# A one-core attention and expert kernel: the order of its first loads and of its first two batches rewritten

## The chip, the core and the metric

The kernel runs on one core of one Trainium2 chip. TensorE (PE in the rows) multiplies matrices into PSUM, VectorE (DVE), ScalarE (ACT) and GpSimd (POOL) compute, and SyncE (SP), ScalarE and GpSimd issue DMAs. Each engine works through its own list of instructions in the order in which the program wrote them, and waits on semaphores for the others. The metric is the device time of one execution in microseconds (us). Before the change it was 331.68 us, the median of three runs that span 331.52 to 332.45.

## The reference, cut to what matters

```python
q, k, v: (8, 12, 448, 64)                       # batch, heads, tokens, head_dim
q_n, k_n = rmsnorm(q, g_q), rmsnorm(k, g_k)     # x / sqrt(mean(x*x) + 1e-6) * g
scores = q_n @ k_n.T / sqrt(64)                 # 448 x 448 for each head
attn = softmax(scores)
x = (attn @ v) -> rows of 12 heads * 64: (3584, 768)
e = token_ids * 2654435761 % 8                  # expert of each token
out[token] = relu(x[token] @ w1[e]) @ w2[e]     # w1 768 x 1024, w2 1024 x 768
```

## The kernel before, in words

The attention runs as 48 steps: 8 batches of 6 steps, and a step (s) is two heads that lie 6 apart in their batch. For a step TensorE makes four pieces of transposed scores (`sc:s.0` to `sc:s.3`; the first three are 128x896, the last 128x448), ScalarE exponentiates each (`exp:s.j`, lines 660 and 663), TensorE multiplies with v (`av:s.0` to `av:s.2`), and VectorE takes reciprocals and scales (`rec`, `x`). Steps 1 and 2, 3 and 4, 6 and 7 and so on share one unit of preparation; steps 0 and 5 are prepared alone.

Preparation of a unit: squares of q and k (`sqq`, `sqk`, line 375 on VectorE; with the mark `@A` line 373 on ScalarE), sums of the squares by TensorE against an identity (`sumq`, `sumk`, line 387), the rest of the sum on VectorE (`redq`, `redk`, line 402), a logarithm and an exponential on ScalarE that give the inverse root (`ln` line 406, `er` line 412), the normalizing product on VectorE (`nq`, `nk`, line 435), transposes on TensorE (`Tq`, `Tk`, lines 595 to 607) and the copy out of PSUM into `qT` and `kT` (lines 623 to 629; `@A` puts it on ScalarE). Squares, sums and inverse roots are made by groups of units: group 0 is step 0, group 1 steps 1 and 2, group 2 steps 3, 4 and 5, groups 3 and 4 are batch 1 (steps 6, 7 and steps 8 to 11), group 5 is batch 2. `v:c` (line 444) copies a chunk of v into the form that `av` reads; chunk 0 is step 0, chunk 1 steps 1 and 2, chunk 2 steps 3 to 5.

PSUM has three double banks `sc_ps` that score pieces take in turn, one bank `qkT_ps`, and the `av_ps` banks. Sums and transposes go to `qkT_ps`, or with the mark `@S` to an `sc_ps`; a bank's next user waits until the last reader of the one before is done.

Loads: q, k and v of step 0 and step 5 come as float32 (step 0 through SP, ACT and POOL; step 5 through SP), all else through POOL's queue as a cast to 16 bits. `load_pairs` (line 317) loads q or k of one unit or one batch in one DMA; `load_v(s, n)` (line 306) loads v of n steps in four DMAs, of which the two with 256 elements a row have 96 KB and the two with 192 elements 72 KB for three steps. Eight of POOL's DMAs can be under way: each waits for the landing of the eighth before it, as its semaphores show.

The order of the first two batches is a text of tokens that `emit` reads from left to right; each token appends its instructions to the lists of the engines that it needs. So the text sets the order on every engine at once. From batch 2 on, another text (`steady`) is used six times over, and after attention come the eight experts. `spin:n` is n idle multiplies of 448 columns of zeros (line 827) into a bank that nobody reads.

```python
        emit("""
            zero:0 zero:1 zero:2 zero:6 zero:7 spin:11 sqk:0.0 zero:3 sqq@A:0.0 sumk@S:0.0
            redk:0.0 sumq@S:0.0 ln:0.1.2 redq:0.0 er:0.1.2 ln:0.0.1 er:0.0.1 sqk@A:1.0
            ...
        """, None)
```

Of the kernel before, what the change touches and what calls it, by code (L numbers as in the profile page):

```python
# [20 lines left out]
def kernel(  # L21
# [243 lines left out]
    with tc.manual_schedule(), \  # L265
# [640 lines left out]
        emit("""
            zero:0 zero:1 zero:2 zero:6 zero:7 spin:11 sqk:0.0 zero:3 sqq@A:0.0 sumk@S:0.0
            redk:0.0 sumq@S:0.0 ln:0.1.2 redq:0.0 er:0.1.2 ln:0.0.1 er:0.0.1 sqk@A:1.0
            gain:0 spin:2 nk:0 spin:4 gain:1 Tk@S:0 nq:0 sumk@S:1.0 gain:2 sqq:1.0 Tq@S:0
            redk:1.0 sumq:1.0 kT:0 redq:1.0 qT@A:0 sc:0.0 ln:1 er:1 sc:0.1 spin:5 exp:0.0  # L910
            nk:1 Tk@S:1 sc:0.3 nq:1 Tq:1 sqk:2.0.0 kT:1 qT:1 exp:0.1 sqq:2.0.0 v:0
            sqk@A:2.0.1 sc:0.2 exp:0.3 sumk@S:2.0 sc:1.0 sqq@A:2.0.1 exp:0.2 exp:1.0
            sumq:2.0 redk:2.0 av:0.0 redq:2.0 sc:1.2 av:0.1 v:1 sc:1.3 ln:2 er:2 av:0.2
            sc:1.1 nq:3 rec:0 exp:1.2 exp:1.3 Tq@S:3 exp:1.1 nk:3 sc:2.0 Tk:3 x:0 exp:2.0
            sc:2.1 exp:2.1 qT:3 kT:3 sc:2.2 av:1.0 exp:2.2 sc:2.3 av:1.1 av:1.2 sqk:3.0
            sc:4.0 exp:2.3 nk:5 sumk:3.0 rec:1 exp:4.0 sc:3.0 x:1 sc:3.1 av:2.0 redk:3.0
            av:2.1 sqk:4.0 exp:3.0 nq:5 sumk:4.0 v:2 sc:3.2 av:2.2 redk:4.0 sqq:3.0 rec:2
            exp:3.1 Tk@S:5 sc:3.3 kT:5 x:2 sumq:3.0 exp:3.2 sc:4.3 sc:4.2 exp:3.3 redq:3.0
            exp:4.3 ln:3 er:3 sc:4.1 exp:4.2 av:3.0 sqk:4.1 Tq:5 exp:4.1 sqq:4.0 av:3.1 qT:5
            sumk@S:4.1 nq:6 av:3.2 nk:6 redk:4.1 sc:5.0 rec:3 sumq:4.0 sc:5.3 sc:5.1 exp:5.0  # L920
            exp:5.3 redq:4.0 sqq:4.1 x:3 Tk:6 exp:5.1 Tq@S:6 kT:6 sumq@S:4.1 redq:4.1 qT@A:6
            av:4.0 av:4.1 ln:4 sc:5.2 av:4.2 er:4 exp:5.2 sc:6.0 sqk:5.0 v:4 sc:7.0 sumk:5.0
            exp:6.0 rec:4 sc:6.3 x:4 av:5.0 av:5.1 exp:7.0 exp:6.3 nq:8 sc:7.3 redk:5.0 nk:8
            exp:7.3 v:3 Tq:8 sc:6.1 av:5.2 qT:8 sc:6.2 Tk@S:8 rec:5 sqq:5.0 exp:6.1 sc:7.1
            sumq:5.0 x:5 exp:6.2 av:6.0 sc:7.2 exp:7.1 exp:7.2 kT:8 sc:8.0 sqq:5.1 redq:5.0
            sc:8.1 nq:10 exp:8.0 av:6.1 sumq:5.1 nk:10 redq:5.1 exp:8.1 av:6.2 sc:8.3 rec:6
            Tk:10 x:6 sc:9.0 sc:8.2 exp:8.3 av:7.0 sc:9.3 exp:9.0 kT:10 Tq:10 av:7.1 av:7.2
            sc:9.1 sqk:5.1 qT:10 exp:8.2 rec:7 sc:9.2 x:7 v:5 exp:9.3 exp:9.1 sumk:5.1
            redk:5.1 exp:9.2 sqq:6.0 av:8.0 av:8.1 av:8.2 sc:10.0 sc:10.2 sc:10.1 rec:8 ln:5
            er:5 x:8 nk:12 exp:10.0 sumq:6.0 av:9.0 exp:10.1 sc:10.3 redq:6.0 Tk:12 av:9.1  # L930
            nq:12 av:9.2 kT:12 rec:9 exp:10.2 sc:11.0 exp:10.3 exp:11.0 sc:11.2 exp:11.2
            sc:11.3 x:9 Tq:12 sqq:6.1 av:10.0 av:10.1 sc:11.1 qT:12 nk:14 av:10.2 exp:11.3
            sc:12.0 sumq:6.1 sc:12.2 rec:10 exp:11.1 sc:12.1 x:10 exp:12.0 exp:12.2 redq:6.1
            Tk:14 sc:12.3 sqk:6.0 exp:12.1
        """, None)
# [407 lines left out]
```

## Time and profile before

| | before |
|---|---|
| median of the runs | 331.68 us (331.52 to 332.45, 3 runs) |
| the profiled execution | 332.74 us |
| its span in the trace | 331.1 us |
| TensorE matmul busy | 318.2 us, 96% of the span |
| VectorE busy | 239.3 us, 72% |
| ScalarE busy | 207.5 us, 63% |
| bytes moved by DMA | 65.52 MB, mean 198 GB/s |
| granted TensorE clock, mean | 0.994 |

The span runs from the first to the last instruction of the core; 1.6 us of the profiled execution lie around it. Attention fills the span until about 159 us, the experts the rest. Every time below is counted from the start of the span. The profiled execution is 1.06 us longer than the median of the runs.

### The profile page before, as it was taken

To read this page: it belongs to the slowest core of one execution; us is meant where nothing else is said; L and a number is where in the kernel's file an instruction comes from. 1 tells how busy PE (TensorE), PEld (TensorE's weight loads), DVE (VectorE), ACT (ScalarE), POOL (GpSimd) and SP (SyncE) were. 2 spreads that over 40 slices of the span, in tenths; PEclk is the share of its full clock that TensorE was granted. 3 is DMA by queue.
4 is the path that set the end of the run, shared out by engine and by line. 5 is a ranking of instruction groups with operands and counts; after the bars stand their busy time and mean duration, and the time that the engine had idled before them with its cause. 6 is when DMAs were issued, how large, how long until landed. Compare 5 with 4: busy or idle time off the path is not lost. (4 is left out here: it accounts for less than half of the span.)

```text
span 331.1 us, 8985 instructions
## 1 busy us (share of the span) xinstructions
PE 318.2 (96%) x3765; PEld 219.7 (66%) x3765; DVE 239.3 (72%) x457; ACT 207.5 (63%) x317; POOL 149.5 (45%) x207
## 2 busy tenths in 40 slices
...
GB/s 122 197 202 203 194 242 196 236 200 240 203 240 212 245 225 227 164 70 70 124 152 211 165 207 242 244 264 265 265 272 239 254 253 260 307 174 137 23 48 124
DMA packets 45601, 65.52 MB, mean 198 GB/s; under 512 B 12727, under 2 KB 33423, under 8 KB 45432
## 3 DMA queue, kind: packets, MB, share of 16 engines
...
q10 hardware_dynamic: 160, 0.11, 0.1%
...
## 5 line engine op out<-in xcount | busy, mean ns | idle before, releaser
L660 ACT ACTIVATE expT<-sc_ps 128x896 bf16<-128x896 f32 x144 | 125.1, 960 | 1.0 <-PE sc_ps L637 0.7
L1072 DVE STREAM_TRANSPOSE xT<-kr 32x768 f16<-32x768 f16 (+1 forms) x80 | 73.6, 920 | 25.7 <-DMA kr<-x_scratch,gidx 15.2
L1024 PEld LDWEIGHTS <-h_sb 128*128 128x128 f16 (+1 forms) x512 | 52.2, 104 | 31.3
L1024 PE MATMUL o_ps<-w_sb,h_sb 128*128 128x512 f16 (+3 forms) x384 | 64.2, 326 | 0.0
L1011 ACT ACTIVATE h_sb<-h_ps 128x480 f16<-128x480 f32 (+1 forms) x56 | 31.3, 560 | 48.6 <-PE h_ps L1002 48.6
L1037 POOL DMA_INDIRECT out_dram<-o_sb,gidx x32 | 35.1, 1097 | 57.6 <-ACT o_sb L1034 29.6
L1034 ACT COPY o_sb<-o_ps 128x768 f32<-128x768 f32 (+1 forms) x26 | 20.8, 799 | 54.5 <-PE o_ps L1024 54.5
L230 POOL DMA_INDIRECT kr<-x_scratch,gidx x32 | 32.6, 1020 | 49.3 <-DVE qT L629 37.1
L1002 PEld LDWEIGHTS <-w_sb 128*128 128x128 f16 x300 | 39.8, 135 | 16.4 <-issue 0.7
L1002 PE MATMUL h_ps<-xT,w_sb 128*128 128x480 f16 x240 | 49.4, 366 | 0.3 <-DVE xT L1072 0.3
L637 PE MATMUL sc_ps<-qT,kT 64*128 64x448 f16 x288 | 44.4, 356 | 0.5 <-DVE qT L629 0.4
L678 PEld LDWEIGHTS <-expT 128*128 128x128 bf16 x846 | 36.8, 97 | 9.2 <-DVE x_sb L738 4.4
L678 PE MATMUL av_ps<-v,expT 128*128 128x65 bf16 x828 | 41.5, 193 | 0.1
L306 POOL DMA_DIRECT2D vr<-in_v_dram x36 | 23.7, 670 | 20.8 <-DMA kr<-in_k_dram 11.5
L738 DVE TENSOR_TENSOR x_sb<-av_ps,srec 128x448 f16<-128x448 f32 x47 | 29.3, 623 | 1.3
L663 ACT ACTIVATE expT<-sc_ps 128x448 bf16<-128x448 f32 x48 | 28.4, 595 | 0.1
L387 PEld LDWEIGHTS <-ident 128*128 128x128 f16 x576 | 22.6, 98 | 8.7 <-issue 4.4
L683 PE MATMUL av_ps<-v,expT 128*128 128x130 bf16 x138 | 24.0, 220 | 0.0
L1024 PE MATMUL o_ps<-kr,h_sb 128*128 128x512 f16 (+3 forms) x128 | 21.1, 326 | 0.0
L1002 PE MATMUL h_ps<-xT,qr 128*128 128x480 f16 x96 | 19.8, 366 | 0.5 <-DVE xT L1072 0.5
L637 PEld LDWEIGHTS <-kT 64*128 64x128 f16 x288 | 12.3, 93 | 9.5 <-issue 2.2
...
## 6 DMA issues: line engine op xcount, KB each, us to landing
...
kr<-in_k_dram POOLq DMA_DIRECT2D x7, 672.0 KB, 15.6
qr<-in_q_dram POOLq DMA_DIRECT2D x7, 672.0 KB, 12.9
...
vr<-in_v_dram POOLq DMA_DIRECT2D x14, 192.0 KB, 13.6
```

The source lines that it names most:

```text
L230: nc.gpsimd.indirect_dma_start(out=xg[0:idx.shape[0], :], out_offset=None, in_=x_dram[0:rows, :], in_offset=bass.IndirectOffsetOnAxis(ap=i ...
L637: nc.tensor.matmul(sc[:, hh, :S], lhsT=kT[64 * hh:64 * hh + 64, P * j:P * j + P], rhs=qT[64 * hh:64 * hh + 64, :], start=True, stop=True)
L660: nc.scalar.activation(expT[:, 2 * j:2 * j + 2, :], sc[:, :, :S], AF.Exp, bias=0.0, scale=1.0)
L663: nc.scalar.activation(expT[:, 6, :], sc[:, 0, :S], AF.Exp, bias=0.0, scale=1.0)
L678: nc.tensor.matmul(av[:, 2 * t + hh, :], lhsT=expT[:, tl(hh, j), P * t:P * t + P], rhs=v8[:, i, vs(hh, j), 0:D + 1], start=(hh == 0 and t ...
L683: nc.tensor.matmul(av[:, 2 * t:2 * t + 2, :], lhsT=expT[:, 6, P * t:P * t + P], rhs=v8[:, i, 0::7, 0:D + 1], start=False, stop=False)
L738: nc.vector.tensor_tensor(out=xs[b][:, :, hp * D:hp * D + D], in0=av[:, :, :D], in1=srec[:, :, None].to_broadcast([P, SL, D]), op=ALU.mult)
L1002: nc.tensor.matmul(dst, lhsT=w1v[:, co, fo, :], rhs=src, start=(co == 0), stop=(co == CO - 1))
L1011: nc.scalar.activation(h_sb[:, fo, c0:c1], h_ps[:, :c1 - c0], AF.Relu)
L1024: nc.tensor.matmul(o_ps[d0 > 0][0:w, d0:d1], lhsT=h_sb[:, fo, col * P:col * P + w], rhs=w2_sb[:, fo, d0:d1], start=(fo == 0), stop=(fo == ...
L1037: scat = nc.gpsimd.indirect_dma_start(out=out[:, :], out_offset=bass.IndirectOffsetOnAxis(ap=idx[0:w], axis=0), in_=o_sb[0:w], in_offset=N ...
L1072: nc.vector.transpose(out=dst[32 * m:32 * m + 32, :, g].rearrange("p c k r -> p k c r"), in_=xg[32 * i:32 * i + 32, 0:n, m])
```

## The change

Three things are rewritten, all in the text between the first load and the second batch's end; no instruction's arithmetic is changed.

1. POOL's first loads: q of steps 1 and 2 goes ahead of the identity that POOL builds, and k and q of steps 3 and 4 go ahead of v of steps 0 to 2 (`load_v(0, 3)`).
2. The token text of batches 0 and 1: the same tokens in another order. Some change engine or bank: the squares of step 0's q go from ScalarE to VectorE; step 0's kT goes from VectorE to ScalarE and its qT the other way, and the same for steps 6 and 7; the bank of several sums and transposes changes. In batch 1 the tokens of k's squares stand further back beside what else is done.
3. Idle multiplies: 14, 7 and 5 in place of 11, 2, 4 and 5.

```diff
         load_pairs(k, k_bufs, 0, 1, 0, HP, 2)
+        load_pairs(q, q_bufs, 0, 1, 0, HP, 2)
         make_identity(nc, ident16[:])
-        load_pairs(q, q_bufs, 0, 1, 0, HP, 2)
-        load_v(0, 3)
         load_pairs(k, k_bufs, 0, 3, 2 * PAIR, HP, 2)
         load_pairs(q, q_bufs, 0, 3, 2 * PAIR, HP, 2)
+        load_v(0, 3)
         load_v(3, 3)
...
-            zero:0 zero:1 zero:2 zero:6 zero:7 spin:11 sqk:0.0 zero:3 sqq@A:0.0 sumk@S:0.0
+            zero:0 zero:1 zero:2 zero:6 zero:7 spin:14 sqk:0.0 sqq:0.0 gain:0 sumk@S:0.0
...
```

POOL's list, from k of steps 1 and 2 to v of steps 0 to 2, is this before (`kr_0`, `qr_0` and `vr_0` are the buffers of k, q and v; 128x2x448 is one unit):

```order
L317 DMA kr_0_68<-in_k_dram 128x2x448
masks.py:197 MEMSET ident16_75 128x128
masks.py:199 AFFINE_SELECT ident16_75<-ident16_75 128x128
L317 DMA qr_0_67<-in_q_dram 128x2x448
L306 DMA vr_0_143<-in_v_dram 64x3x256
L306 DMA vr_0_143<-in_v_dram 64x3x192 x2
L306 DMA vr_0_143<-in_v_dram 64x3x256
L317 DMA kr_0_68<-in_k_dram 128x2x448
L317 DMA qr_0_67<-in_q_dram 128x2x448
```

and this after:

```order
L317 DMA kr_0_68<-in_k_dram 128x2x448
L317 DMA qr_0_67<-in_q_dram 128x2x448
masks.py:197 MEMSET ident16_75 128x128
masks.py:199 AFFINE_SELECT ident16_75<-ident16_75 128x128
L317 DMA kr_0_68<-in_k_dram 128x2x448
L317 DMA qr_0_67<-in_q_dram 128x2x448
L306 DMA vr_0_143<-in_v_dram 64x3x256
L306 DMA vr_0_143<-in_v_dram 64x3x192 x2
```

The loads of steps 3 and 4 have passed the four of v; what comes after them in the queue is the same.

VectorE's list, from the squares of q of steps 1 and 2 to the first copy of v, is this before:

```order
L375 TENSOR_TENSOR sq_q_359<-qr_0_67 128x14x16x4
L402 TENSOR_REDUCE ss_366<-sc_ps_341 128x14
L626 TENSOR_SCALAR kT_385<-sc_ps_334,g_col_78 128x512
L402 TENSOR_REDUCE ss_366<-qkT_ps_368 128x14
L435 TENSOR_TENSOR n8_k_147<-kr_0_68,rr_394 128x2x7x64
L435 TENSOR_TENSOR n8_q_146<-qr_0_67,rr_394 128x2x7x64
L375 TENSOR_TENSOR sq_k_427<-kr_0_68 128x14x16x4
L626 TENSOR_SCALAR kT_429<-sc_ps_407,g_col_78 128x1024
L629 COPY qT_431<-qkT_ps_419 128x896
L375 TENSOR_TENSOR sq_q_434<-qr_0_67 128x14x16x4
L444 COPY v8_145<-vr_0_143 128x8x64
L402 TENSOR_REDUCE ss_483<-sc_ps_442 128x22
```

and this after:

```order
L375 TENSOR_TENSOR sq_q_363<-qr_0_67 128x14x16x4
L629 COPY qT_370<-sc_ps_365 128x448
L402 TENSOR_REDUCE ss_372<-sc_ps_346 128x14
L435 TENSOR_TENSOR n8_q_146<-qr_0_67,rr_398 128x2x7x64
L435 TENSOR_TENSOR n8_k_147<-kr_0_68,rr_398 128x2x7x64
L375 TENSOR_TENSOR sq_k_409<-kr_0_68 128x14x16x4
L629 COPY qT_453<-sc_ps_416 128x896
L375 TENSOR_TENSOR sq_q_457<-qr_0_67 128x14x16x4
L402 TENSOR_REDUCE ss_460<-qkT_ps_433 128x22
L626 TENSOR_SCALAR kT_462<-sc_ps_424,g_col_78 128x1024
L444 COPY v8_145<-vr_0_143 128x8x64
```

Step 0's copy out is now that of qT; the copies of steps 1 and 2 come q first, with the squares of q of steps 3 and 4 between them; the copy of v stays last here.

ScalarE's list around its first exponentials is this before (`expT_404` is step 0, `expT_464` step 1):

```order
L660 ACTIVATE expT_404<-sc_ps_390 128x896
L660 ACTIVATE expT_404<-sc_ps_396 128x896
L373 ACTIVATE sq_k_427<-kr_0_68 128x8x16x4
L663 ACTIVATE expT_404<-sc_ps_416 128x448
L373 ACTIVATE sq_q_434<-qr_0_67 128x8x16x4
L660 ACTIVATE expT_404<-sc_ps_438 128x896
L660 ACTIVATE expT_464<-sc_ps_459 128x896
L406 ACTIVATE ss_483<-ss_483 128x2x22
L412 ACTIVATE rr_515<-ss_483 128x2x44
L660 ACTIVATE expT_464<-sc_ps_496 128x896
```

and this after (`expT_400` is step 0, `expT_504` step 1):

```order
L660 ACTIVATE expT_400<-sc_ps_393 128x896
L373 ACTIVATE sq_k_409<-kr_0_68 128x8x16x4
L660 ACTIVATE expT_400<-sc_ps_411 128x896
L373 ACTIVATE sq_q_457<-qr_0_67 128x8x16x4
L660 ACTIVATE expT_400<-sc_ps_450 128x896
L663 ACTIVATE expT_400<-sc_ps_455 128x448
L406 ACTIVATE ss_460<-ss_460 128x2x22
L412 ACTIVATE rr_502<-ss_460 128x2x44
L660 ACTIVATE expT_504<-sc_ps_485 128x896
L663 ACTIVATE expT_504<-sc_ps_500 128x448
```

The logarithm and inverse root of steps 3 to 5 now stand ahead of step 1's first exponential.

## Rows read from the trace of the kernel before

**Rows 1.** Busy time by stretch: length, each engine's busy us, clock, DMA share, GB/s

```profile
25.00:35.00 10.00, 10.00 (x217) 7.60 (x214) 9.89 (x25) 9.88 (x17) 9.59 (x25) 1.00 1.35 201
60.00:80.00 20.00, 20.00 (x368) 14.54 (x365) 18.67 (x39) 20.00 (x33) 6.81 (x10) 1.00 1.28 231
```

**Rows 2.** Timeline of ScalarE: start us, us, what, xcount [idle before it <- releaser]

```profile
12.31 0.23 ACT L406 ACTIVATE ss<-ss 128x28 f32<-128x28 f32 x1 [1.87 <-DVE ss L402]
12.72 1.71 ACT L660 ACTIVATE expT<-sc_ps 128x896 bf16<-128x896 f32 x2
...
17.17 0.92 ACT L660 ACTIVATE expT<-sc_ps 128x896 bf16<-128x896 f32 x1 [0.46 <-PE sc_ps L637]
...
18.75 0.90 ACT L660 ACTIVATE expT<-sc_ps 128x896 bf16<-128x896 f32 x1
...
19.97 3.34 ACT L660 ACTIVATE expT<-sc_ps 128x896 bf16<-128x896 f32 x4
23.16 0.59 ACT L663 ACTIVATE expT<-sc_ps 128x448 bf16<-128x448 f32 x1
23.58 3.40 ACT L660 ACTIVATE expT<-sc_ps 128x896 bf16<-128x896 f32 x4
...
54.89 0.61 ACT L663 ACTIVATE expT<-sc_ps 128x448 bf16<-128x448 f32 x1
```

**Rows 3.** Timeline of VectorE, the same columns

```profile
7.57 1.28 DVE L435 TENSOR_TENSOR n_one<-expT,rr 128x512 f16<-128x512 f32 x2
...
10.77 0.63 DVE L375 TENSOR_TENSOR sq_q<-qr 128x896 f16<-128x896 f16 x1 [1.85 <-DMA qr<-in_q_dram]
...
11.44 0.47 DVE L626 TENSOR_SCALAR kT<-sc_ps,g_col 128x512 f16<-128x512 f16 x1
...
12.85 0.63 DVE L435 TENSOR_TENSOR n_k<-kr,rr 128x896 f16<-128x896 f16 x1 [0.57 <-ACT rr L412]
...
14.69 0.63 DVE L375 TENSOR_TENSOR sq_k<-kr 128x896 f16<-128x896 f16 x1 [0.68 <-DMA kr<-in_k_dram]
15.23 0.75 DVE L626 TENSOR_SCALAR kT<-sc_ps,g_col 128x1024 f16<-128x1024 f16 x1
15.89 0.61 DVE L629 COPY qT<-qkT_ps 128x896 f16<-128x896 f16 x1
16.42 0.62 DVE L375 TENSOR_TENSOR sq_q<-qr 128x896 f16<-128x896 f16 x1
16.95 0.29 DVE L444 COPY v<-vr 128x512 bf16<-128x512 bf16 x1
17.16 0.24 DVE L402 TENSOR_REDUCE ss<-sc_ps 128x22 f32<-128x88 f32 x1
...
18.87 0.63 DVE L435 TENSOR_TENSOR n_q<-qr,rr 128x896 f16<-128x896 f16 x1 [0.28 <-ACT rr L412]
```

**Rows 4.** Timeline of VectorE, squares of batch 2's k

```profile
32.51 0.96 DVE L375 TENSOR_TENSOR sq_k<-kr 128x1344 f16<-128x1344 f16 x1
```

**Rows 5.** Timeline of TensorE, the first idle multiplies

```profile
1.41 4.29 PE L827 MATMUL av_ps<-hi 128*128 128x448 f16 x11 [1.41 <-DVE hi L806]
```

**Rows 6.** Timeline of GpSimd: issues of q (steps 1, 2) and v (steps 0 to 2)

```profile
4.26 0.74 POOL L317 DMA_DIRECT2D qr<-in_q_dram  x1
4.99 2.48 POOL L306 DMA_DIRECT2D vr<-in_v_dram  x4
```

**Rows 7.** DMA issues at 4.26, 7.40, 8.12, 8.85, 18.13: KB each, us to landing

```profile
qr<-in_q_dram POOLq DMA_DIRECT2D x1, 224.0 KB, 6.5
...
kr<-in_k_dram POOLq DMA_DIRECT2D x1, 224.0 KB, 7.3
...
qr<-in_q_dram POOLq DMA_DIRECT2D x1, 224.0 KB, 7.7
...
vr<-in_v_dram POOLq DMA_DIRECT2D x1, 96.0 KB, 7.2
...
kr<-in_k_dram POOLq DMA_DIRECT2D x1, 672.0 KB, 13.5
```

More of the change, by code (lines that the diff above doesn't have):

```diff
@@ L906 @@
         emit("""
-            zero:0 zero:1 zero:2 zero:6 zero:7 spin:11 sqk:0.0 zero:3 sqq@A:0.0 sumk@S:0.0
[L908 to L924, printed above, removed]
@@ L931 @@
[L931 to L934, printed above, removed]
+            zero:0 zero:1 zero:2 zero:6 zero:7 spin:14 sqk:0.0 sqq:0.0 gain:0 sumk@S:0.0
+            zero:3 redk:0.0 sumq:0.0 gain:1 ln:0.1.2 redq:0.0 ln:0.0.1 spin:7 er:0.1.2
+            gain:2 er:0.0.1 nk:0 nq:0 sqk@A:1.0 Tk:0 sumk@S:1.0 sqq:1.0 Tq@S:0 qT:0 redk:1.0
@@ new lines @@
+            sumq@S:1.0 kT@A:0 sc:0.0 redq:1.0 ln:1 er:1 exp:0.0 nq:1 spin:5 nk:1 sqk:2.0.0
+            sc:0.2 sqk@A:2.0.1 exp:0.2 Tq@S:1 Tk@S:1 sumk:2.0 sc:0.1 qT:1 sc:0.3 sqq:2.0.0
+            sqq@A:2.0.1 redk:2.0 kT:1 sumq:2.0 v:0 exp:0.1 redq:2.0 exp:0.3 sc:1.0 av:0.0
+            v:1 ln:2 sc:1.3 er:2 exp:1.0 av:0.1 av:0.2 nq:3 sc:1.2 nk:3 rec:0 Tq:3 sc:1.1
+            qT:3 exp:1.3 exp:1.2 sc:2.0 exp:1.1 exp:2.0 sc:2.3 x:0 nk:5 v:2 Tk:3 exp:2.3
+            av:1.0 sc:2.1 exp:2.1 av:1.1 av:1.2 kT:3 sc:2.2 sc:3.0 sc:3.2 sqk:3.0 sumk:3.0
@@ new lines @@
+            exp:2.2 rec:1 x:1 redk:3.0 exp:3.0 sc:3.1 nq:5 av:2.0 av:2.1 av:2.2 sqk:4.0
+            Tq@S:5 rec:2 exp:3.2 sc:4.0 x:2 exp:3.1 Tk:5 exp:4.0 qT:5 kT:5 sc:4.2 sumk@S:4.0
+            av:3.0 sc:3.3 exp:4.2 sqq:3.0 sqk:4.1 exp:3.3 redk:4.0 sumq:3.0 redq:3.0 sqq:4.0
+            ln:3 sc:5.0 sc:5.2 av:3.1 sumq@S:4.0 er:3 nq:6 sumk:4.1 exp:5.0 exp:5.2 sqq:4.1
+            sc:4.1 redk:4.1 av:3.2 sumq:4.1 sc:4.3 redq:4.0 nk:6 rec:3 redq:4.1 Tk@S:6 x:3
+            Tq:6 sqk:5.0 exp:4.1 sc:5.3 av:4.0 exp:4.3 av:4.1 ln:4 kT@A:6 qT:6 er:4 sc:5.1
@@ new lines @@
+            av:4.2 sc:6.0 exp:5.3 nq:8 exp:5.1 sc:6.2 rec:4 nk:8 sumk:5.0 exp:6.0 x:4
+            exp:6.2 Tq@S:8 av:5.0 redk:5.0 sc:6.3 v:3 av:5.1 sc:7.0 exp:6.3 qT:8 sc:6.1
+            sc:7.1 exp:7.0 av:5.2 exp:6.1 sqq:5.0 nq:10 rec:5 x:5 sumq:5.0 exp:7.1 Tk@S:8
+            redq:5.0 sc:7.2 av:6.0 av:6.1 kT:8 sqq:5.1 sc:7.3 exp:7.2 av:6.2 sc:8.0 sc:8.1
+            exp:7.3 exp:8.0 sumq:5.1 rec:6 exp:8.1 nk:10 sc:8.2 x:6 redq:5.1 v:4 sc:9.0
+            av:7.0 sqk:5.1 Tk:10 av:7.1 kT:10 exp:8.2 av:7.2 sc:8.3 sc:9.3 Tq:10 rec:7
```

13 lines of the change are left out of this document (7 added, 6 removed).

## The prediction, made before the changed kernel was run

> **What bounds the kernel now.** I read the busy time by stretch first. From 60 to 80 us, in the steady part of attention, ScalarE is busy 20.00 of 20 us: its exponentials follow each other without a gap [rows 1]. Its timeline gives the pace: four large exponentials start in 23.16 - 19.97 = 3.19 us, 0.80 us each, and a small one takes 23.58 - 23.16 = 0.42 us [rows 2]. The change leaves the texts of batches 2 to 7 and the experts alone, so what it wins or loses is how much sooner or later ScalarE gets to the end of batch 1's work. I use the exponential that starts at 54.89 us, the first of the steady text, as the mark [rows 2]; a shift there is carried to the end one to one, because the experts follow attention.
>
> Between the first exponential at 12.72 us and the mark there are two kinds of lost time. First, in the start-up ScalarE stands visibly: 1.87 us before 12.31 and 0.46 us before 17.17 [rows 2]. Second, from 23.58 to 54.89 us it has no visible gap, yet it runs below its pace: 30 large and 9 small exponentials, the logarithms and roots of three groups (0.41 + 0.55 + 0.56 us by the same timeline) and one copy of qT (0.79) need 24.0 + 3.78 + 2.31 = 30.09 us and took 31.31, so 1.22 us went into short waits for scores. In that stretch VectorE is busy 9.89 of 10 us, ScalarE 9.88 [rows 1]: both are full, and a late copy of kT or qT shows as a late score.
>
> VectorE's timeline says why the start is late: it waits 1.85 us for q of steps 1 and 2, which lands at 4.26 + 6.5 = 10.76 us, and 0.68 us for k of steps 3 and 4, which lands at 7.40 + 7.3 = 14.7 [rows 3, 7].
>
> **The change part by part.** *Start of the first exponential.* It needs step 0's scores and, in ScalarE's order, the root of steps 1 and 2, which needs q of these steps. Before: landing 10.76, squares 10.77, sums, reduction, logarithm 12.31, exponential 12.72 [rows 2, 3]. After, q is issued one identity earlier, 0.58 us (4.26 back to 3.68, where k's issue ends). But it queues behind k of steps 1 and 2 in the same queue, and step 5's loads share the engines, so I take no earlier landing; the bound on the good side is the whole 0.58 us. The 14 idle multiplies last 14 x 0.39 = 5.46 us from 1.41, to 6.87, against 5.70 before (4.29 us for 11) [rows 5]; step 0's first sum, ready at 6.2, waits some 0.6 us for them, and with step 0's second square now in VectorE's line its norms end at about 9.6 to 9.9 instead of 8.85 (7.57 + 1.28) [rows 3]. That is hidden under the landing at 10.76; were q to land 1 us earlier it would bind. The 7 multiplies end near 9.5 and delay only transposes that have until 11. Copying qT after q's squares, 11.35 to 11.8, replaces the copy of kT at 11.44 [rows 3]. First exponential: 12.72, shift 0 (0 to -0.58).
>
> *From there to step 1.* I add VectorE's new list with the old durations, by start-to-start times: norms of steps 1 and 2 from 12.85 as before, two at 0.55; squares of k of steps 3 and 4 at 13.95, because k now lands before it; copy of qT 14.5 (0.53); squares of q 15.05 (0.53); reduction 15.6 (0.2, with its sum on TensorE perhaps 15.8); kT 16.0 (0.66); v 16.65 (0.21); second reduction 16.9 to 17.1 [rows 3]. Logarithm and root take 0.41 us (12.31 to 12.72) [rows 2], so step 1's first exponential starts at 17.5 and its second at 18.3. Before, the first started at 17.17, but logarithm and root came after it and the second started at 18.75 [rows 2]. ScalarE itself had its step 0 work done by 17.17 - 0.46 = 16.71, so VectorE's chain ends last in both. The gain is 18.75 - 18.35 = 0.40 us; bounds 0 (one more bank wait: piece 1 of step 0 takes the bank that piece 2 leaves) and 0.7.
>
> *When do the loads land?* Before, k and q of steps 3 and 4 landed at 14.7 and 15.8, the next v piece at 16.05, in the order of issue [rows 7]. After, q of steps 1 and 2, these two and v's four pieces are the same bytes, 224 + 224 + 336 KB after 10.76, so the last of them lands near 15.8 whichever order they have; by share, k at 10.76 + 5.04 x 224/784 = 12.2, q at 13.6, v at 15.8. k and q are in time (13.95, 15.05). v is needed at 16.65: 0.85 us to spare, cost nothing.
>
> *Up to the mark.* The norm of q of steps 3 and 4 starts at 17.65 instead of 18.87 [rows 3], so VectorE is 1.2 us ahead, ScalarE 0.4. With VectorE ahead, fewer scores are late: of the 1.22 us of short waits I take half back, 0.6. Bounds: all 1.22 us; or 0.6 us more than before, since a new order can place its own short waits.
>
> Here the Trainium skill has a rule (Perfetto Trace Analysis, Identifying the Most-Contended Engine): matmul busy share says little about TensorE, the share of LDWEIGHTS more. The row has 10.00 of 10 us for matmuls and 7.60 for weights [rows 1]. Read by the first, TensorE is the bound of this stretch and this term would be 0; by the rule it has room and the term stands. The trace alone doesn't decide, so 0 lies inside my bounds.
>
> *VectorE can't run ahead for long.* The squares of batch 2's k start at 32.51, and that k lands at 18.13 + 13.5 = 31.6 [rows 4, 7]. With 1.2 us of lead, and the copy of kT of steps 6, 7 gone from ahead of it, VectorE would be there near 30.9 and wait 0.7. Then the copy of qT for step 6 is done by 33.1, just before ScalarE's place for it (before: 34.2 less the gain). Cost nothing; uncovered it would be 0.5.
>
> *Moved copies.* ScalarE now copies kT of steps 6 and 7 (1024 elements) instead of qT (896): 128 x (0.80 - 0.42)/448 = +0.11 us. Step 0's squares leave it where it was idle: 0.
>
> *Sum.* 0 - 0.40 - 0.60 + 0.11 = -0.89 us. Against the profiled execution: 332.74 - 0.89 = 331.85. That execution is 1.06 above the median of the runs, so the median goes from 331.68 to 330.8.
>
> **Rivals.** *The lead is lost (no change).* TensorE or the new order puts as many short waits back, or loads do not land by order of issue. For it: three engines are full at once [rows 1]. Against: VectorE's 0.68 us wait for k plainly goes if k lands first. If k of steps 3 and 4 lands at 14.7 as before, VectorE stands from 13.95 to 14.7, and 0.75 us later everything above it is: 0 + 0.35 - 0.60 + 0.11 = -0.14, so 331.5. The rule beside it in the Trainium skill (DMA: Bandwidth & Descriptors, Two DMAs through the same engine are not ordered) says that nothing orders transfers across the 16 engines; the rows in issue order speak the other way here.
>
> *All of it (faster).* q lands 0.58 sooner and every short wait goes: -0.58 - 0.40 - 1.22 + 0.11 = -2.09, so 329.6. For it: VectorE's lead is nearly as large as the waits. Against: 30.09 us of work without a gap is more than ScalarE shows anywhere at its steady pace.
>
> *v comes late (slower).* v's copy stands in VectorE's list ahead of the reduction that step 1's exponentials wait for. If the last of v's pieces lands after 16.65, each us is one us of the whole kernel; from 17.55 on it eats the gain. The last piece will be issued near 9.0 (four take 2.48 us [rows 6], from 6.5). With the 7.2 us of the next v piece it lands at 16.2; with 10 us, which lies between that and the 13.5 of a load in a full queue [rows 7], at 19.0: +2.35 - 0.89 = +1.5, so 333.1. Against: the bytes ahead of it, above.
>
> **How the numbers follow.** A measurement of this kernel tells 0.3%, 1.0 us, from no change. Forecast 0.47 (330.8; its own range 330.1 to 331.4), lead lost 0.26 (331.5), all of it 0.15 (329.6), v late 0.12 (333.1). Faster by over 1.0 us: all of the third and 0.21 of the forecast's 0.47, 0.36. Slower: v late and a little of the second, in which a worse order costs over 1 us, 0.14. The same: 0.50. The range reaches into both sides, 329.5 to 332.3; v late lies outside.
>
> **What would show it.** VectorE's wait for `kr` at 14.69 gone, its squares of k near 14; first exponential at 12.2 to 12.8; step 1's second exponential near 18.3; the v copy without a DMA wait before it; the first steady exponential near 54.0; steady batches at the old pace. A DMA wait before the v copy, or a ScalarE total from the second exponential to the mark as long as before, would make it wrong.

## The result, and the profile after

The changed kernel takes 334.40 us (median of 5 runs, 333.43 to 334.83) against 332.19 of the kernel before in the same series (331.52 to 332.73): ratio 1.0062, 95% interval 1.0037 to 1.0087. A later repeat, with 12 runs of it against 35 of the kernel before, gave 1.0031 (1.0003 to 1.0059). It is slower, by 1 to 2 us. The profiled execution of the changed kernel took 334.83 us, its span is 332.9.

The steady part is as it was; the loss lies ahead of it. By stretch, answering to [rows 1] with the same columns, and then us by us where the clock falls:

```profile
25.00:35.00 10.00, 8.30 (x177) 6.19 (x176) 7.93 (x21) 8.48 (x15) 9.52 (x23) 0.94 1.34 202
60.00:80.00 20.00, 20.00 (x373) 14.81 (x371) 18.57 (x40) 20.00 (x30) 5.13 (x8) 1.00 1.29 226
...
32.00:33.00 1.00, 0.07 (x6) 0.09 (x1) 0.67 (x1) 0.91 (x2) 0.93 (x3) 1.00 1.26 205
33.00:34.00 1.00, 0.23 (x2) 0.11 (x3) 1.00 (x3) 0.00 (x0) 0.94 (x6) 0.93 1.29 207
34.00:35.00 1.00, 1.00 (x11) 0.41 (x8) 1.00 (x4) 0.68 (x1) 1.00 (x2) 0.50 1.42 193
35.00:36.00 1.00, 1.00 (x16) 1.00 (x14) 0.47 (x2) 1.00 (x2) 0.94 (x5) 0.50 1.57 190
36.00:37.00 1.00, 1.00 (x16) 1.00 (x15) 0.99 (x3) 0.04 (x1) 0.90 (x2) 0.50 1.52 192
```

Before, VectorE and ScalarE were busy 9.9 of the 10 us from 25 to 35; now 7.93 and 8.48. TensorE does almost nothing from 32 to 34, and its granted clock, 1.00 all through this part before, is 0.50 (the 1.2 GHz level) from 34 to 37.

ScalarE's timeline, answering to [rows 2]: the start-up is earlier than in the recorded execution of before, and then two waits stand where there was none.

```profile
11.09 0.23 ACT L406 ACTIVATE ss<-ss 128x28 f32<-128x28 f32 x1 [0.72 <-DVE ss L402]
11.51 0.90 ACT L660 ACTIVATE expT<-sc_ps 128x896 bf16<-128x896 f32 x1
...
16.55 0.90 ACT L660 ACTIVATE expT<-sc_ps 128x896 bf16<-128x896 f32 x1
...
34.32 1.73 ACT L660 ACTIVATE expT<-sc_ps 128x896 bf16<-128x896 f32 x2 [1.41 <-PE sc_ps L637]
37.49 0.54 ACT L663 ACTIVATE expT<-sc_ps 128x448 bf16<-128x448 f32 x1 [1.45 <-PE sc_ps L640]
...
56.77 0.56 ACT L663 ACTIVATE expT<-sc_ps 128x448 bf16<-128x448 f32 x1
```

The last line is the prediction's mark: 54.89 before, 56.77 now, +1.88. VectorE and TensorE show where it comes from, answering to [rows 3, 4]. The single row behind them is the copy of step 6's qT in the kernel before, which stood on ScalarE:

```profile
9.37 0.62 DVE L375 TENSOR_TENSOR sq_q<-qr 128x896 f16<-128x896 f16 x1
...
12.71 0.62 DVE L375 TENSOR_TENSOR sq_k<-kr 128x896 f16<-128x896 f16 x1
...
15.26 0.66 DVE L444 COPY v<-vr 128x512 bf16<-128x512 bf16 x1
...
32.33 0.86 DVE L375 TENSOR_TENSOR sq_k<-kr 128x1344 f16<-128x1344 f16 x1 [1.97 <-DMA kr<-in_k_dram]
33.11 0.62 DVE L629 COPY qT<-qkT_ps 128x896 f16<-128x896 f16 x1
```

```profile
33.77 0.88 PE L637 MATMUL sc_ps<-qT,kT 64*128 64x448 f16 x4 [1.70 <-DVE qT L629]
34.59 1.30 PE L387 MATMUL qkT_ps<-sq_k,ident 128*128 128x84 f16 x16
```

```profile
32.05 0.94 ACT L623 ACTIVATE qT<-sc_ps 128x896 f16<-128x896 f16 x1
```

The chain reads: the squares of batch 2's k wait 1.97 us for its landing; behind them in VectorE's list stands the copy of step 6's qT; step 6's scores wait for it (1.70 us on TensorE), ScalarE waits for the scores (1.41). Then TensorE works at half clock: its 16 sums take 1.30 us, and the next scores are late as well (1.45). Where I wrote ahead of the prediction that k's squares stand further back in batch 1's text, the reverse holds for those of batch 2's k: the token `sqk:5.0` stood behind `qT@A:6` and `sc:6.0`, and now stands ahead of `qT:6`.

GpSimd's issues, answering to [rows 6], and batch 2's k, the fifth load of [rows 7], say why k is late:

```profile
3.68 0.77 POOL L317 DMA_DIRECT2D qr<-in_q_dram  x1
...
4.98 0.72 POOL L317 DMA_DIRECT2D kr<-in_k_dram  x1
5.70 0.72 POOL L317 DMA_DIRECT2D qr<-in_q_dram  x1
6.38 3.73 POOL L306 DMA_DIRECT2D vr<-in_v_dram  x6
11.54 0.61 POOL L306 DMA_DIRECT2D vr<-in_v_dram  x1 [1.43 <-DMA kr<-in_k_dram]
13.28 0.61 POOL L306 DMA_DIRECT2D vr<-in_v_dram  x1 [1.14 <-DMA qr<-in_q_dram]
14.12 0.85 POOL L317 DMA_DIRECT2D kr<-in_k_dram  x1 [0.23 <-DMA vr<-in_v_dram]
```

```profile
kr<-in_k_dram POOLq DMA_DIRECT2D x1, 672.0 KB, 13.7
```

Each load waits for the landing of the eighth before it. The last two v loads of batch 0 are now eight behind k and q of steps 3 and 4, stand until these have landed, and hold back batch 1's k (672 KB), issued at 14.12. Batch 2's k lands at 18.57 + 13.7 = 32.3.

### The profile page after: what moved, and what is told of

It reads as the page before. It is cut to its first block, busy times and chain, and to the rows that moved or that the text cites. A ratio compares the mean times of both kernels' runs of the same rounds, so it can differ in the third digit from the quotient of the medians.

```text
span 332.9 us, 8994 instructions
## 1 busy us (share of the span) xinstructions
PE 320.8 (96%) x3769; PEld 222.1 (67%) x3769; DVE 240.4 (72%) x458; ACT 206.9 (62%) x316; POOL 148.9 (45%) x207
## 5 line engine op out<-in xcount | busy, mean ns | idle before, releaser
L1105 POOL DMA_DIRECT2D w_sb<-in_moe_w_dram x20 | 13.7, 693 | 10.1 <-DMA w_sb<-in_moe_w_dram 7.5
```

## The experiments

Times to before are ratios with 95% intervals. Beside them I use one account, worked out from ScalarE's timeline of each profiled execution: batch 2's first root (line 406, 128x84) comes at the first exponential plus ScalarE's idle gaps (those over 0.15 us, which the timeline prints) plus the rest. The rest is called work, but shorter waits are in it too.

| kernel | first exp | idle | work | root | ratio to before |
|---|---|---|---|---|---|
| before, as recorded | 12.72 | 0.66 | 32.70 | 46.08 | |
| before, repeated | 10.98 | 0.88 | 32.70 | 44.56 | 0.9992 (0.9976 to 1.0009) |
| changed | 11.51 | 3.53 | 32.94 | 47.98 | 1.0062 (1.0037 to 1.0087) |
| changed, repeated | 11.50 | 2.87 | 32.88 | 47.25 | 1.0031 (1.0003 to 1.0059) |
| squares later | 11.50 | 1.69 | 33.05 | 46.24 | 1.0016 (0.9994 to 1.0039) |
| batch 2's k sooner | 11.39 | 1.56 | 33.08 | 46.03 | 1.0003 (0.9980 to 1.0026) |
| old loads, changed text | 12.27 | 1.16 | 32.62 | 46.05 | 1.0016 (0.9992 to 1.0039) |
| changed loads, old text | 10.64 | 2.27 | 33.58 | 46.49 | 0.9993 (0.9971 to 1.0014) |
| clock held | 11.63 | 2.74 | 32.83 | 47.20 | 1.0041 (1.0025 to 1.0057) |
| k squares from batch 1 | 11.84 | 1.31 | 32.88 | 46.03 | 1.0008 (0.9989 to 1.0027) |
| k and q squares from batch 1 | 11.30 | 1.45 | 32.68 | 45.43 | 1.0022 (1.0003 to 1.0040) |
| q first alone | 11.13 | 1.09 | 32.68 | 44.90 | 1.0000 (0.9977 to 1.0022) |
| batch 1's k ahead | 11.31 | 1.29 | 33.06 | 45.66 | 1.0030 (1.0011 to 1.0048) |
| the same, old opening | 11.03 | 1.34 | 33.12 | 45.49 | 1.0015 (0.9996 to 1.0034) |
| old opening alone | 13.10 | 1.29 | 32.74 | 47.13 | 1.0014 (0.9996 to 1.0033) |
| old loads and opening | 11.84 | 1.67 | 32.77 | 46.28 | 1.0049 (1.0027 to 1.0071) |

One row is one execution; single executions of one kernel lie up to 4.9 us apart on one chip (the kernel before, 331.12 to 336.02), so a row's root and its ratio needn't rank alike.

**Three theories first.** A: the loss is the wait, because the squares of batch 2's k stand ahead of step 6's qT. B: the order costs by itself. C: the moved loads make k late.

*Squares later*: `sqk:5.0` and its sum moved behind step 4's output.

```diff
-Tq:6 sqk:5.0 exp:4.1 ... nk:8 sumk:5.0 exp:6.0 x:4 exp:6.2
+Tq:6 exp:4.1 ... nk:8 exp:6.0 x:4 sqk:5.0 exp:6.2 Tq@S:8 av:5.0 sumk:5.0
```

> The changed kernel with the squares of batch 2's k (sqk:5.0) moved five VectorE instructions back, behind step 4's x, and their sums behind step 5's first product with v. Theory A (the place): these squares stand ahead of step 6's qT and hold it until k lands at 32.3 us; then VectorE's 1.97 us wait shrinks to below 0.5, TensorE's clock stays at full between 33 and 38 us, the first steady exponential starts near 54 us instead of 56.8, and the ratio to before is 0.994 to 0.998. Theory B (the order): the new order of batch 1 is slower by itself, by bank turns and crowded engines; the ratio stays at 1.003 or more although the wait goes.

The DMA wait is gone, the clock stays 1.00, and the root comes 1.74 us sooner than in the changed kernel. The ratio, 1.0016, lies between A's forecast and B's.

*Batch 2's k sooner*: issued ahead of batch 1's v.

```diff
-load(1)
-load(2, "kq")
+load(1, "kq")
+load(2, "k")
+load(1, "v")
+load(2, "q")
```

> The changed kernel with batch 2's k loaded ahead of batch 1's v; the token order is untouched. Theory A: k of batch 2 lands 672 KB of queue sooner, near 29 us, so VectorE finds it there at 30.3, no wait, ratio 0.994 to 0.998 as for the squares moved later. Theory B: ratio 1.003 or more. If batch 1's v, now 3.4 us later (about 30), is missed, a DMA wait shows before its copy at 36 us; I expect none.

No wait at the squares (31.18), the clock 1.00; but VectorE's first v copy waits 1.11 us at 16.21 now. The ratio, 1.0003, again lies between the two.

*Half of the change each*: the loads of before with the changed text, and the changed loads with the text of before.

> The loads of before with the token order and the idle multiplies of the changed kernel. Theory A: q of steps 1 and 2 lands near 10.8 again and the first exponential falls back to 12.5 or later; VectorE reaches batch 2's squares near 31.3 and k lands at 31.6, so that wait is below 1 us; ratio 0.999 to 1.005. Theory B: 1.006 or more. Theory C (the moved loads made batch 2's k late): the wait is gone and the ratio is below 0.998.

> The moved loads with the token order and idle multiplies of before. Theory A: q of steps 1 and 2 lands below 9.6 us as in the changed kernel, VectorE's 0.68 us wait for k of steps 3 and 4 goes, and batch 2's squares come behind enough work to miss nothing: ratio 0.994 to 1.000. Theory C: batch 2's k at 32.3 holds VectorE here too, ratio 1.002 or more.

Neither half shows the loss in its ratio. With the old loads VectorE finds batch 2's k there. With the new ones and the old text it waits 1.53 us for batch 1's k and 1.07 for batch 2's, so the loads make k late under either text. In the profiles A and C hold together: the loads make k late and the changed text comes for it sooner; C's forecast for the ratio of the second half (1.002 or more) failed. B isn't excluded. The old loads with the changed text lose 1.16 us, all of the idle time in that row, at a place where the changed kernel loses 0.24: VectorE waits 0.80 us for k of steps 3 and 4 at 14.36, and step 0's third score stands in TensorE's list behind the sums of those squares.

**What the wait costs, what the clock costs, and a control.** *Clock held*: eight idle multiplies ahead of step 6's scores, a new token.

```diff
-av:4.2 sc:6.0
+av:4.2 hold:8 sc:6.0
```

> The changed kernel with eight idle 448-column multiplies on TensorE ahead of step 6's scores (some 1.5 us at full clock), so that TensorE isn't idle while VectorE waits for batch 2's k. The wait of 1.97 us itself stays. Theory A2 (part of the 1.88 us lost is TensorE's clock, which fell to 0.50 from 34 to 37 us): granted clock 1.00 from 32 to 38, the transposes and sums at 34 to 36 back to 0.8 and 0.55 us, the first root of batch 2 some 0.5 to 1.0 us sooner than the changed kernel's 47.98, ratio to before 1.002 to 1.004. Rival (the clock only stretches work that has nobody waiting; VectorE's wait alone makes the loss): 47.8 to 48.1, ratio 1.006.

```profile
34.00:37.00 3.00, 3.00 (x52) 2.07 (x51) 2.80 (x8) 1.91 (x3) 2.87 (x9) 1.00 1.51 197
```

```profile
33.05 1.69 PE L887 MATMUL sc_ps<-hi 128*128 128x448 f16 x8
34.66 0.55 PE L637 MATMUL sc_ps<-qT,kT 64*128 64x448 f16 x4
```

The granted clock is 1.00 where it was 0.50. ScalarE's waits there are 1.11 and 0.21 us instead of 1.41, 1.45 and 0.21, VectorE's is 1.29; the root comes 0.78 sooner, and the ratio is 1.0041. This doesn't split the loss into wait and clock. The copy of step 6's qT ends at 34.09 and the scores start at 34.66, when the idle multiplies are done, so these cost some 0.5 us themselves. And the changed kernel's repeat, below, has about the same wait (1.40), no idle multiplies, a clock of 1.00 and the same root (47.25).

*k squares from batch 1*: the first half of the squares of batch 2's k reads batch 1's k, which landed long before. The kernel leaves out that half of batch 2's norms; order, loads and number of instructions stay.

```diff
+if gi == 5 and a == 1:
+    t1 = raw_at(k_bufs, 1, 0, 6 * PAIR)...
+    return [[((t1, t)[i][:, i, u0:u0 + n], 0, 7 * n)] for i in range(2)]
 return [[(t[:, i, u0:u0 + n], 0, 7 * n)] for i in range(2)]
```

> The changed kernel in which the first squares of batch 2's k read batch 1's k in their place, which landed long before: order, loads and instruction counts are the changed kernel's, only the wait for the landing is gone. (It leaves out one half of batch 2's k norms.) Theory A (that wait is the whole loss): no wait over 0.5 us on any engine between 30 and 38 us, ScalarE keeps the lead of 1.3 us that the changed kernel has at 34 us, first root of batch 2 at 44.6 to 45.2, ratio to before 0.994 to 0.997. Rival B2 (the order behind it has waits of its own there, as it had with the squares moved back by a few instructions): the lead is gone by 38 us, first root 45.8 to 46.3, ratio 0.999 to 1.001.

The ratio is 1.0008 (0.9989 to 1.0027): no loss is seen, but not the 1 us of gain either that I expected of A. On the same chip this kernel took 332.66 us and the one with the held clock, in which the wait stands, 333.95; some 0.5 of that 1.3 are the idle multiplies. VectorE meets the next load:

```profile
36.13 0.86 DVE L379 TENSOR_TENSOR sq_q<-qr 128x1344 f16<-128x1344 f16 x1 [0.94 <-DMA qr<-in_q_dram]
```

*The same for k and q*, both halves of each, so that batch 2's own norms are left out:

> The changed kernel in which all squares of batch 2's k and q read batch 1's in their place, so that neither landing can hold VectorE (it leaves out batch 2's own norms). In the run with k alone replaced the queue met q of batch 2 next: 0.94 us on VectorE at 36.1, 0.87 on TensorE, 0.53 on ScalarE. Theory D (with both landings gone, the order itself holds): ScalarE's idle time from the first exponential to batch 2's root falls from 1.31 to 0.6 to 0.9 us, root 0.3 to 0.7 us sooner by the first exponential, ratio to before 0.997 to 1.000. Rival (the order has waits of its own): idle time 1.2 or more, ratio as with k alone, 1.001.

No landing stops VectorE from 28 to 43 us; then the next load does, batch 3's q, and 1.18 of ScalarE's 1.45 us idle follow from it:

```profile
43.91 0.86 DVE L379 TENSOR_TENSOR sq_q<-qr 128x1344 f16<-128x1344 f16 x1 [1.11 <-DMA qr<-in_q_dram]
```

Take one landing away and the order runs into the one behind it. The root is 0.60 sooner than with k alone, but the ratio, 1.0022, is no better: in the time, no gain.

*q first alone*: the kernel before, with q of steps 1 and 2 ahead of the identity.

```diff
+load_pairs(q, q_bufs, 0, 1, 0, HP, 2)
 make_identity(nc, ident16[:])
-load_pairs(q, q_bufs, 0, 1, 0, HP, 2)
```

> The kernel before with one edit: q of steps 1 and 2 is issued ahead of the identity, as in the changed kernel. Theory L (the queue's order sets landings beyond the 0.58 us of the issue): q lands by 9.6 instead of 10.76, k of steps 1 and 2 no later than before. Rival (landings move with the issue): 10.1 to 10.2. The first exponential hangs on step 0, so 12.3 to 12.8 either way, and the ratio to before is 0.998 to 1.001 for both.

Ratio 1.0000 (0.9977 to 1.0022). q was there by 9.12, when VectorE came for it. What that says of the queue hangs on the control:

> The kernel before, unchanged, as a control: the time from ScalarE's last steady root (132.03 in the first profile) to the end of attention was 27.42 us there, and 27.13 in the changed kernel, but 28.1 to 28.6 in the four variants run on another chip. If that is the chip or the execution, the control shows 27.9 to 28.6; if it is the changed order giving back its lead at the end, it shows 27.3 to 27.6. Ratio 0.998 to 1.002.

The control upsets the recorded profile's start. VectorE's and ScalarE's timelines of the kernel before, repeated:

```profile
9.03 0.63 DVE L375 TENSOR_TENSOR sq_q<-qr 128x896 f16<-128x896 f16 x1 [0.27 <-DMA qr<-in_q_dram]
...
13.17 0.63 DVE L375 TENSOR_TENSOR sq_k<-kr 128x896 f16<-128x896 f16 x1 [0.90 <-DMA kr<-in_k_dram]
...
30.98 0.90 DVE L375 TENSOR_TENSOR sq_k<-kr 128x1344 f16<-128x1344 f16 x1
```

```profile
10.98 1.71 ACT L660 ACTIVATE expT<-sc_ps 128x896 bf16<-128x896 f32 x2
```

The same q, issued at 4.26 again, is there at 9.03, not 10.76 [rows 3], and the first exponential is at 10.98, not 12.72. So the 1.2 us by which the changed kernel's start beat [rows 2] can't be counted as gain: against the control it starts 0.53 later. Neither execution is the rule. With q issued at 4.26 it landed at 9.0, 9.9 and 10.8 us in the three profiles that tell it, with q issued near 3.68 at 8.5 to 9.8 in eight. From its last steady root (130.42) to the last copy of attention's output, on ScalarE at 158.46, the control takes 28.04 us: the 28.1 to 28.6 of the first four variants is no matter of the changed order. Eleven of the eighteen profiles, both of the changed kernel among them, have 27.1 to 27.2 there.

**Why k is late, and the opening.** *Batch 1's k ahead* of the last four v loads:

```diff
 load_v(0, 3)
+load(1, "k")
 load_v(3, 3)
-load(1)
+load(1, "qv")
```

> The changed kernel with one load issued elsewhere: k of batch 1 (672 KB) ahead of the last four v loads of batch 0, not behind them. In the changed kernel GpSimd issues the last two v loads only when k and q of steps 3 and 4, eight loads ahead of each, have landed (waits of 1.43 and 1.14 us), and batch 1's k stands behind both, so the transfers run thin: 189 and 172 GB/s in 12 to 16 and 16 to 20 us, and 144 to 186 in 16 to 20 in all six kernels with the moved loads, against 201 to 206 in the four with the old ones. Theory Q (that standing makes batch 2's k late): over 190 GB/s in both stretches, batch 2's k lands at least 0.7 us sooner than the changed kernel's 32.3, the wait of 1.97 us on VectorE falls under 1.2, first root of batch 2 at 46.0 to 47.2, ratio to before 1.001 to 1.004; what it can cost is v of steps 3 to 5, which now stands behind 672 KB. Rival (k of batch 2 is late because of the bytes ahead of it, which are the same): lands at 32.0 to 32.8, root 47.7 to 48.2, ratio 1.005 to 1.007.

The transfers from 12 to 16 and 16 to 20 us (last column GB/s), first of the changed kernel, then of its repeat, of the control, and of this one:

```profile
12.00:16.00 4.00, 3.74 (x58) 2.68 (x56) 3.96 (x10) 3.63 (x6) 2.63 (x5) 1.00 1.43 189
16.00:20.00 4.00, 3.82 (x63) 2.68 (x62) 3.56 (x9) 3.87 (x7) 4.00 (x6) 1.00 1.21 172
```

```profile
12.00:16.00 4.00, 3.70 (x56) 2.64 (x55) 3.21 (x7) 3.69 (x6) 2.85 (x4) 1.00 1.41 188
16.00:20.00 4.00, 2.89 (x46) 1.93 (x46) 2.98 (x8) 2.90 (x6) 3.92 (x7) 1.00 1.17 159
```

```profile
12.00:16.00 4.00, 2.79 (x46) 2.02 (x44) 2.98 (x7) 3.32 (x6) 2.47 (x4) 1.00 1.37 197
16.00:20.00 4.00, 4.00 (x67) 2.64 (x63) 3.38 (x8) 3.76 (x7) 3.54 (x5) 1.00 1.27 206
```

```profile
12.00:16.00 4.00, 3.67 (x61) 2.80 (x61) 3.52 (x10) 3.51 (x7) 2.48 (x5) 1.00 1.35 203
16.00:20.00 4.00, 3.81 (x63) 2.54 (x59) 3.54 (x7) 3.97 (x7) 2.30 (x5) 1.00 1.37 197
```

The control moves (197 + 206) x 4 = 1612 KB in these 8 us, the changed kernel 1444, its repeat 1388: 168 to 224 KB too few, which at 206 GB/s are 0.8 to 1.1 us. With batch 1's k ahead it is 1600 again. GpSimd stands even longer (1.06, 1.16, 0.36 and 1.70 us before four v loads) and issues batch 2's k later, at 19.91, but k lands sooner:

```profile
31.37 0.86 DVE L375 TENSOR_TENSOR sq_k<-kr 128x1344 f16<-128x1344 f16 x1 [0.36 <-DMA kr<-in_k_dram]
```

So it isn't the time of issue; what this kernel loses when its queue runs thin comes back when it doesn't. Over all profiles that tell it, batch 2's k lands at 30.7 to 31.6 us in the four with the old loads, at 31.6 to 32.9 in the seven with the moved ones, and at 30.6 to 31.4 in the three with batch 1's k ahead. The root is 2.32 us sooner than in the changed kernel and the clock stays 1.00, as Q had it and more. In the time no gain is shown: the ratio, 1.0030, is that of the changed kernel's repeat, 1.0031. The profiled execution is 1.15 us shorter than the median of its 12 runs, and a v copy now waits 0.97 us at 20.71.

*The opening.* Two kernels put 11 idle multiplies and ScalarE's square of step 0's q back:

```diff
-spin:14 sqk:0.0 sqq:0.0 gain:0 sumk@S:0.0 zero:3
+spin:11 sqk:0.0 sqq@A:0.0 gain:0 sumk@S:0.0 zero:3
```

> As the one with batch 1's k ahead, and the opening put back: 11 idle multiplies in place of 14 ahead of the first sums, and step 0's q squared on ScalarE, not on VectorE behind k. Theory S (the changed opening costs 0.3 to 0.5 us: the first exponential came 3.5 to 3.7 us behind the second root in both kernels, and that root at 7.65 to 7.9 with the changed opening against 7.13 to 7.62 with the old one): second root at 7.2 to 7.5, first exponential at 10.8 to 11.1. Theory Q with S: first root of batch 2 at 45.5 to 46.7, ratio 1.000 to 1.003. Rival (an earlier opening only lengthens the wait for batch 2's k, which lands by the clock): root as without the opening, ratio the same within 0.001.

> The changed kernel with the old opening (11 idle multiplies, step 0's q squared on ScalarE) and the first squares of batch 2's k behind step 4's output, as in the earlier run; the loads stay as changed. Theory: each part is worth what it showed alone; first exponential 10.8 to 11.1, idle time of ScalarE from there to batch 2's root 1.2 to 1.8 us, root at 45.3 to 45.9 against 46.24 without the opening, ratio to before 0.998 to 1.001. Rival (landings decide): root 46.0 to 46.4, ratio 1.000 to 1.003.

Both took 336.9 us, ratios 1.0130 (1.0097 to 1.0163) and 1.0122 (1.0090 to 1.0153). The token `zero:3`, which fills step 5's buffers on ScalarE, now stood behind a square that waits for q, and SyncE's loads of step 5 wait for the fill. SyncE's issue in the second kernel, 3.59 in the changed one, and the wait on ScalarE:

```profile
6.43 2.14 SPq L306 DMA_DIRECT2D kr<-in_k_dram  x3
```

```profile
14.86 0.63 ACT L373 ACTIVATE sq_k<-kr 128x512 f16<-128x512 f32 x1 [2.96 <-DMA kr<-in_k_dram]
```

The edit was misplaced, and the runs say nothing of the opening; they show what one token ahead of another costs. With `zero:3` ahead of the square, in three more runs:

> The changed kernel with the old opening alone, the zero fills of step 5's buffers ahead of ScalarE's square this time (in the two runs before it they stood behind it, and SyncE's loads of step 5 were issued at 6.43 in place of 3.59). Theory S (the opening costs 0.3 to 0.5 us): second root at 7.2 to 7.5 against 7.81, first exponential 10.8 to 11.1. What it is worth in the end: by theory Q batch 2's k lands by the loads, whenever the opening ends, so the wait in VectorE grows by what the opening gained (2.0 to 2.4 us) and the first root of batch 2 stays at 47.5 to 48.1, ratio 1.005 to 1.007. Rival (the opening is worth its 0.4 us): root 47.2 to 47.6, ratio 1.0045 to 1.0055.

> Batch 1's k ahead of the last four v loads, and the old opening. Theory Q and S together account for the loss: first exponential 10.8 to 11.1, ScalarE idle 1.0 to 1.6 us from there to the first root of batch 2 (1.29 with k ahead alone), root 45.0 to 45.6, ratio to before 1.000 to 1.003. Rival (a third part is missing, in the order of batch 1): root 45.6 or later, ratio 1.003 or more.

> The loads and the opening of the kernel before, with the changed order of batches 0 and 1 behind them: the order alone. Rate of the transfers over 190 GB/s in 12 to 16 and 16 to 20 us, batch 2's k there when VectorE comes (no wait over 0.3 us). Theory (the order is worth nothing by itself): first exponential 10.8 to 11.3 where q of steps 1 and 2 lands by 9.3, idle time of ScalarE to batch 2's root 0.9 to 1.3, root 44.6 to 45.4, ratio 0.999 to 1.002. Rival (the order costs by itself): idle time over 1.5 or root over 45.6, ratio over 1.002.

In the profile of the old opening alone, the norm gain landed late (VectorE waits 1.27 us for it at 7.20) and the clock was 0.57 from 8 to 12 us. Its first exponential is at 13.10, 1.6 us behind the repeat's 11.50, and yet its root, 47.13, is level with 47.25: what the start loses, the wait for k gives back, since VectorE finds batch 2's k there at 32.78. Its ratio, 1.0014, is below what either theory had (1.0045 to 1.007). With batch 1's k ahead as well, the first exponential is at 11.03 and the root at 45.49, within the expected 45.6; ratio 1.0015. Its profiled execution was even so the longest of its 12 (335.25 us, median 333.20). From the last copy of attention's output to the end it took 175.1 us, where the kernel with k ahead alone took 172.0, and a root doesn't see that. The third went against me: its rate (204 GB/s in 16 to 20) and its missing wait for batch 2's k are as expected, but its ratio is 1.0049, where the same kernel with the changed opening had 1.0016. Idle time (1.67), root (46.28) and ratio all fall to the rival, that the order costs by itself. The profile has part of the reason. q landed late (0.51 us of wait), and then ScalarE stands for the same score as with the old loads and the changed opening, because k of steps 3 and 4 is late for the changed order:

```profile
14.04 0.63 DVE L375 TENSOR_TENSOR sq_k<-kr 128x896 f16<-128x896 f16 x1 [0.91 <-DMA kr<-in_k_dram]
```

```profile
15.86 0.92 ACT L660 ACTIVATE expT<-sc_ps 128x896 bf16<-128x896 f32 x1 [1.28 <-PE sc_ps L637]
```

That doesn't explain why the two medians differ by 0.3%.

*The changed kernel again*:

> The changed kernel, unchanged, as a control on this chip: ratio to before 1.004 to 1.009 again; transfers under 190 GB/s in 16 to 20 us; VectorE's wait for batch 2's k 1.2 to 2.2 us; granted clock under 1.00 somewhere in 33 to 38 us where TensorE has been idle over 1.5 us; first root of batch 2 at 47.2 to 48.2. If the loss were one of the first chip alone, the ratio would be under 1.003.

```profile
32.90 0.88 DVE L375 TENSOR_TENSOR sq_k<-kr 128x1344 f16<-128x1344 f16 x1 [1.40 <-DMA kr<-in_k_dram]
```

```profile
34.36 0.56 PE L637 MATMUL sc_ps<-qT,kT 64*128 64x448 f16 x4 [1.16 <-DVE qT L629]
```

The wait and the thin stretch are back, the slower clock isn't: TensorE stood 1.16 us, not 1.70, and was granted 1.00 from 32 to 39 us. So the fall of the clock is a part that some executions have. The same 16 sums take 0.78 us here, and from step 6's first score on TensorE to ScalarE's small exponential of step 6 it is 2.52 us, where it was 3.72 at half clock; ScalarE's waits for this chain are 0.72, 0.39 and 0.21 us, not 1.41, 1.45 and 0.21. The ratio, 1.0031, is under the 1.004 that I expected, and hardly above the 1.003 under which I would have put the loss down to the first chip. Another part of the idle time is new, VectorE's first copy of v:

```profile
16.58 0.29 DVE L444 COPY v<-vr 128x512 bf16<-128x512 bf16 x1 [1.37 <-issue]
```

```profile
17.06 0.24 ACT L406 ACTIVATE ss<-ss 128x44 f32<-128x44 f32 x1 [1.19 <-DVE ss L402]
```

```profile
vr<-in_v_dram POOLq DMA_DIRECT2D x1, 96.0 KB, 8.3
```

The last line is the last piece of v of steps 0 to 2, issued at 8.20; it lands at 16.5, the copy follows at once, and ScalarE stands 1.19 us for the reduction behind it. So in this execution the late v costs about as much as the late k.

## Why the prediction was wrong

By the account, the changed kernel against the control: 0.53 us by the first exponential, 3.53 - 0.88 = 2.65 by idle time, 0.24 by ScalarE's work, together 3.42. The end of attention is 160.87 against 158.46, and the span 332.9 against 330.6: 2.3 of it are left, since the control loses 0.9 in its last stretch (28.04 us against 27.13). The median of 334.40 us lies above the range of 329.5 to 332.3, and the sign is wrong as well.

- *"VectorE can't run ahead for long"*, priced *"Cost nothing"*, is the step that failed. I had the place, the squares of batch 2's k, and a wait of 0.7 us, and let the copy of step 6's qT finish just in time. VectorE came at 30.36, not 30.9, k landed at 32.3, not 31.6, so the wait was 1.97 us, and the copy of qT ended at 33.73, not 33.1. ScalarE had come to step 6 at 32.91, 1.3 us ahead of the kernel before, and what was behind the wait was covered by nothing: ScalarE stood 1.41 us at once, and 1.45 more when TensorE fell to half clock. I priced the wait and not the list behind it. In the repeat the same chain cost 0.72 + 0.39 + 0.21 = 1.32 us.
- *"When do the loads land?"* looked at the loads of steps 1 to 4 alone, *"the same bytes"* in another order. The last piece of v of steps 0 to 2 I put near 9.0, and it was issued at 8.20; the v of steps 3 to 5 behind it I did not follow. By the rule of eight, which was in the listing, its last two pieces had to wait for k and q of steps 3 and 4, which land at 12.2 and 13.6 by my own numbers, with batch 1's k behind. The loads of batches 1 and 2 had no line in my sum, other than the landing of batch 2's k, taken over at 31.6.
- *The first exponential* (0, to -0.58): against [rows 2] it came 1.21 us sooner, against the control 0.53 later. I had written that the longer opening would bind "were q to land 1 us earlier"; in the changed kernel it did: VectorE came to q's squares at 9.37 behind step 0's norms and had no wait. The start-up was read from gaps that another execution doesn't have.
- *The short waits* (-0.60) were there, and the new order has them too. In the recorded kernel these two exponentials start 1.11 us apart where 0.80 is the pace, and TensorE made the score for the second in between:

```profile
38.24 0.99 ACT L660 ACTIVATE expT<-sc_ps 128x896 bf16<-128x896 f32 x1
```

```profile
39.35 0.92 ACT L660 ACTIVATE expT<-sc_ps 128x896 bf16<-128x896 f32 x1
```

  Added up from the first exponential to the root, where no idle time is printed, the starts that follow an exponential lie later than the fastest pace (0.797 and 0.424 us) by 1.04 us there, 1.05 in the control, 0.97 in the changed kernel and 0.79 in its repeat. So 0.1 to 0.3 of the forecast 0.60 came. They are part of the work column, which is 32.70 in both profiles of the kernel before and 32.94 and 32.88 in the two of the changed one.
- *Moved copies* (+0.11): ScalarE's copy of kT takes 1.00 us until the next start (30.38 to 31.38), that of qT before took 0.79, so +0.21.
- *From there to step 1* and *the loads of steps 3 and 4* held in the first profile: squares of k at 12.71 (forecast 13.95, with a first exponential 1.2 later), no wait, step 1's second exponential at 17.35. ScalarE's idle time up to there is 0.46 us against 0.88 in the control, the 0.40 of the forecast. In the repeat the late v took this and more: that exponential is at 18.31.
- *Rivals.* The slower one was a late v. Its mechanism, a landing that VectorE meets with all else queued behind it, is what happened, in the first profile with batch 2's k some 16 us later, in the repeat with both: v landed at 16.5, near the 16.2 of my first estimate, and VectorE was there for it at 15.2, not at 16.65.

Open: how the loss divides in the time. The waits are shown in the profiles, and with batch 2's k taken out of the way no loss is seen (1.0008). But medians of 12 runs are sure to 0.2% or 0.3% only: the interval of the changed kernel's repeat overlaps those of most kernels without the wait, batch 1's k ahead has the repeat's ratio, and the old loads with the old opening, without that wait, came out at 1.0049. That the order costs by itself is not excluded. No version was clearly faster than the kernel before.
